# Bonus products from PSUM one step earlier, third convolution tile by full diagonals, and a reordered prologue in an RWKV-5 plus gated-convolution kernel

## The chip, the cores and the metric

The kernel runs on one core of a Trainium2 chip. The metric is device time in microseconds (us): the median over several executions. A profile of one execution gives its span, from the first to the last instruction, and the time of each instruction on the engines PE (TensorE, with PEld for its weight loads), DVE (VectorE), ACT (ScalarE), POOL (GpSimd) and SP (SyncE, which here only issues DMAs).

## What is computed

Two stages in fp32 at the edges: linear attention with a decaying state (B = 4 batches, H = 8 heads, S = 768 tokens, D = 48 per head), then a gated unit with a causal convolution over 5 tokens on the 384 concatenated channels.

```python
# attention, per token t
cur = einsum('bhd,bhe->bhde', u * k_t, v_t)          # the bonus
y_t = einsum('bhd,bhde->bhe', r_t, state + cur)
state = w * state + einsum('bhd,bhe->bhde', k_t, v_t)
# gated unit on x = y with heads concatenated: (4, 768, 384)
gate = sigmoid(sum_k conv_w[k] * shift(x, k))        # depthwise, causal, 5 taps
out = (gate * (x @ w_val)) @ w_out
```

## The kernel before

**Units.** Tokens are handled in chunks of 128, two chunks (256 tokens) to a unit, three units to a batch: 12 units. Decay within a chunk is folded into r and k: `dr` and `dk` hold powers of w, computed on ACT in the prologue as exp(scale x ln w). `scale_r` (L221) multiplies r by `dr`, one pair of heads of a whole batch at a time (POOL, in the prologue partly DVE); `scale_k` (L241) multiplies k of a unit by `dk` (POOL). PE transposes both: `transp_r` (L230) for one pair and one batch, `transp_k` (L256) for one unit, each into one of two PSUM buffers `tr_ps`, from which ACT (or DVE) copies to `rT` and `kT`.

**A step.** The order of all instructions is written out by hand in a loop of 13 steps (L511). Step i works on attention of unit i and on the gated unit of f = i - 1. Each engine executes its instructions in this order, one after the other. In step i:

- loads are issued on SP (k and v of unit i + 3; r of a later batch in steps 0, 2 and 5);
- `y_out(f)` (L364): the attention output of unit f on PE, transposed, from the state `z`, the masked scores `at` and the bonus term `dv`; ACT copies it to `xT`;
- `cast_v`, `scale_k` for unit i + 1 (ACT, POOL);
- `prod(i)` (L273): DVE multiplies `rT` by `kT`, both bf16 in SBUF, for the bonus of unit i;
- `attn(i, 0)` (L301): scores of the first chunk; `mask_at` (L318) on DVE; `bonus(i)` (L277): eight small matmuls that reduce the product, and a DVE copy to `s`; `bonus_v` (L293): POOL forms `dv` from v and `s`; `state` and `decay` (L327, L353): the new state on PE and its decay on DVE;
- `scale_r` of pairs of the next batch on POOL, by a small plan (L535): in most steps a pair is scaled one step before it is transposed, except in steps 1 and 2;
- `conv(f)` (L405), `value(f)` (L430) of the gated unit, with DVE's product `hT`;
- `attn(i, 1)`, its mask, state and decay;
- `transp_r` of one pair, `transp_k(i + 1)`, `project(f)` (L459) with ACT's copies `o_sb` and the output DMA, `transp_r` of a second pair.

**The gated unit.** The depthwise convolution is done on PE as matmuls with diagonal matrices. The 384 channels are three tiles of 128. Before, all diagonals are 64x64 (`cwdiag`), so four matmuls work at once on the quarters of the array: tiles 0 and 1 over 256 tokens, then tile 2 with its two chunks side by side (128 columns each). The two halves of a tile end up swapped by `qo = (q + i) % 2`, and the weights `wval` and `wout` are stored in a matching order: four column groups, tile 2 twice. Gate, value and `hT` are then two pieces of 384 columns. PSUM buffers for all of this come from a ring of three, `mm_ps`.

**The prologue.** It issues loads on SP (w, r of batch 0, k and v of the first units, the weights), small loads of w and u on POOL's queue, builds the identity and the mask on POOL, computes the decay factors on ACT, and lets PE multiply the identity 60 times (L492). Then it prepares unit 0: `scale_r`, `scale_k`, the transposes, `uw2` and `wcm` on DVE. The diagonals (`prep_conv`, L192) and the weights (`cast_weights`, L211) are prepared at the end of step 0.

Of the kernel before, what the change touches and what calls it, by code (L numbers as in the profile page):

```python
# [16 lines left out]
def kernel(  # L17
# [69 lines left out]
    nc.sync.dma_start(out=w_bc, in_=w.partition_broadcast(128))  # L87
    load_r(0)
    load_kv(0, "kv")
    load_kv(1, "k")  # L90

    nc.scalar.preload_act_table_set("natural_log_exp_and_others")
# [4 lines left out]
    for dst, src in ((wt, w), (ut, u)):  # L97
        for par in range(2):
            nc.gpsimd.dma_start(
                out=dst[64 * par : 64 * par + D, :],  # L100
                in_=src.rearrange("(p two) d -> two d p", two=2)[par],
            )

# [5 lines left out]
    ident = consts.tile([128, 128], BF16)  # L109
    make_identity(nc, ident)  # L110
# [18 lines left out]
    nc.scalar.activation(out=dk, in_=lnw_bc, func=AF.Exp, scale=sc_k)  # L129
    dr = consts.tile([128, H, J, D], F32)  # L130
    for j in range(J):
        nc.scalar.activation(
            out=dr[:, :, j, :], in_=lnw_bc, func=AF.Exp, scale=sc_r[:, j : j + 1]
        )
# [3 lines left out]
    nc.scalar.preload_act_table_set("sigmoid_and_others")  # L138
# [33 lines left out]

    wv_st = consts.tile([128, NT, DM], F32)
    wo_st = consts.tile([128, 4, DM], F32)
    cw5 = consts.tile([KW, DM], F32)

    def load_weights():
        nc.sync.dma_start(out=cw5, in_=moe_conv_w)
        nc.sync.dma_start(out=wv_st, in_=moe_w_val.rearrange("(t p) n -> p t n", p=128))
        wo = moe_w_out.rearrange("(t p) n -> p t n", p=128)  # L180
        nc.sync.dma_start(out=wo_st[:, 0::2, :], in_=wo[:, 0::2, :])
        nc.sync.dma_start(out=wo_st[64:128, 1::2, :], in_=wo[0:64, 1:3, :])
        nc.sync.dma_start(out=wo_st[0:64, 1::2, :], in_=wo[64:128, 1:3, :])

    wval = consts.tile([128, NT, 4, 128], BF16)
    wout = consts.tile([128, 4, DM], BF16)
    cw5b = consts.tile([KW, DM], BF16)
    cwT = consts.tile([128, NT, KW], F32)
    cwdiag = consts.tile([128, NT, KW, 64], BF16)
    eye = consts.tile([128, 64], BF16)  # L190

    def prep_conv():  # L192
# [10 lines left out]
        for T in range(NT):  # L203
            nc.vector.tensor_tensor(
                out=cwdiag[:, T],
# [3 lines left out]
            )  # L209

    def cast_weights():  # L211
        wv = wv_st.rearrange("p k (t x) -> p k t x", x=128)
        nc.gpsimd.tensor_copy(wval[:, :, 0::2, :], wv[:, :, 0::2, :])
        nc.gpsimd.tensor_copy(wval[:, :, 1::2, 64:128], wv[:, :, 1:3, 0:64])
        nc.gpsimd.tensor_copy(wval[:, :, 1::2, 0:64], wv[:, :, 1:3, 64:128])
        nc.scalar.copy(out=wout, in_=wo_st)
# [39 lines left out]
    def transp_k(n):  # L256
# [10 lines left out]
        )  # L267

# [4 lines left out]
    def prod(n):  # L273
        st["pr", n] = wk.tile([128, NP, W], BF16, name="pr")
        nc.vector.tensor_tensor(out=st["pr", n], in0=rTu(n), in1=st["kT", n], op=ALU.mult)  # L275
# [129 lines left out]
    def conv(n):  # L405
        b, cu = divmod(n, NU)
        xT, t0 = xT_t[b % 2], cu * W
        gate = ffn.tile([128, 2, W + C], BF16, name="gate")
        g_ps = [ps_mm.tile([128, W + C], F32, name="mm_ps") for i in range(2)]
        for T0 in (0, 2):  # L410
            for t in range(KW):
                for q in range(2):
                    for i in range(2):
                        T = 2 if T0 else i
                        c0, n0, o0 = (i * C, C, W) if T0 else (0, W, 0)
                        rows = slice(64 * q, 64 * q + 64)
                        qo = (q + i) % 2
                        nc.tensor.matmul(  # L418
                            out=g_ps[i][64 * qo : 64 * qo + 64, o0 : o0 + n0],
                            lhsT=cwdiag[rows, T, t, :],  # L420
                            rhs=xT[rows, T, t0 + c0 + t : t0 + c0 + t + n0],
                            start=(t == 0 and T0 == 0),
                            stop=(t == KW - 1),
# [164 lines left out]
```

## Time and profile before

| | |
|---|---|
| median of 13 runs (lowest to highest) | 119.01 us (118.57 to 120.05) |
| profiled execution: its time, its span | 118.78 us, 116.9 us |
| DVE product `pr` (L275), 12 times | 12.7 us, 0.68 to 2.24 each |
| DVE mask product (L320), 24 times | 29.2 us, 1.22 each |
| PE convolution (L418), 480 matmuls | 13.1 us busy |
| PE value (L437 and L446), 144 matmuls | 20.9 us busy |
| POOL `rs` (L223), 14 times | 20.5 us, 1.48 each |
| POOL waiting for `s_sb` from DVE | 35.7 us, 12 times |
| DMA, whole execution | 20.77 MB |

How to read it: a row of the timeline gives start, duration, engine, line and operation, then output and inputs with partitions x elements and type, then in brackets how long the engine had been idle and what ended that. Consecutive instructions of a kind are merged with their number. A wait row gives the total, the number and the longest. A stage row gives busy time and number of instructions per engine, the share of full clock that was granted to PE, the busy share of the DMA engines and their rate. The columns between the brackets and the shares stand in the order PE, PEld, DVE, ACT, POOL. Busy time of single PE instructions overlaps, since matmuls are pipelined; the start-to-start distance says what they cost.

Steps of the profiled execution begin (first matmul of `y_out`) at 22.73 (step 1), 34.98, 43.12, 50.30, 57.60, 65.35, 72.52, 79.82, 87.56, 94.80, 101.34 and 107.45 (step 12).

### The profile page before, as it was taken

The page shows a single profiled execution, that of the slowest core. Times are in us where ns is not written, and L with a number is a line of the kernel's source. Part 1 is how long each engine was busy: PE and PEld are TensorE (multiplying, and loading weights), DVE is VectorE, ACT ScalarE, POOL GpSimd, SP SyncE. Part 2 cuts the span into 40 slices and gives each one's busy share as a digit, 9 for nine tenths or more (in the row PEclk, how much of TensorE's full clock was granted, in tenths as well). Part 3 has the DMA queues.
Part 4 walks back from the last instruction along what each step waited for, and adds up shares of the span by engine and source line. Part 5 has one row for each costly group of instructions (what it writes and reads, how often), then busy time and mean ns, then how long its engine had stood idle before and what let it go on. Part 6 is the DMA issues. An engine that isn't in the chain of part 4 may idle for free.

```text
span 116.9 us, 5086 instructions
## 1 busy us (share of the span) xinstructions
PE 95.5 (82%) x2247; PEld 74.2 (63%) x2247; DVE 76.9 (66%) x122; ACT 69.1 (59%) x123; POOL 65.2 (56%) x62
## 2 busy tenths in 40 slices
PE   0397255867999698999979989998898999999860
PEld 0396233645778486768857776776776868776620
DVE  0508769898276717797797289977774778967030
ACT  4399250491259387393874964749669386644540
POOL 6948551962970990957939549299491825022000
PEclk9999965555599999999999999999999999999999
DMA  1899999899998999968869798993965003030303
GB/s 44 214 291 192 220 337 199 161 259 336 182 189 214 310 238 241 223 148 196 161 181 370 157 257 179 234 216 76 232 127 163 8 0 140 0 139 2 140 0 135
DMA packets 58719, 20.77 MB, mean 178 GB/s; under 512 B 50501, under 2 KB 58698, under 8 KB 58698
## 3 DMA queue, kind: packets, MB, share of 16 engines
q1 hardware_dynamic: 58570, 20.46, 72.2%
q8 instruction: 17, 0.28, 1.1%
q0 software_dynamic: 128, 0.00, 0.2%
q14 instruction: 4, 0.03, 0.1%
HBM read 15.74 MB, written 4.72 MB: 175 GB/s over the span
## 4 chain that ended last, share of the span: by engine, by line
PE 39%; SPq 15%; issue 12%; DVE 11%; ACT 9%; POOL 7%; DMA 3%; DVEq 0%; POOLq 0%; ACTq 0%
SPq L72 11%; PE mm_ps L418 8%; PE mm_ps L437 6%; DVE pr L275 6%; PE mm_ps L374 5%; PE mm_ps L466 5%; ACT kT L265 4%; POOL rs L223 3%; DMA k_st<-in_k_dram 3%; POOL ks L242 3%; DVE hT L454 3%; PE at_ps L308 3%; ACT o_sb L473 3%; PE mm_ps L282 3%; PE kv_ps L334 2%
## 5 line engine op out<-in xcount | busy, mean ns | idle before, releaser
L294 POOL TENSOR_TENSOR dv<-v_st,s_sb 128x768 bf16<-128x768 f32 x12 | 17.7, 1475 | 35.7 <-DVE s_sb L291 35.7
L320 DVE TENSOR_TENSOR at<-at_ps,mask 128x1024 bf16<-128x1024 f32 x24 | 29.2, 1218 | 3.0 <-PE at_ps L308 2.7
L454 DVE TENSOR_TENSOR hT<-mm_ps,gate 128x384 bf16<-128x384 f32 x24 | 13.4, 558 | 13.0 <-PE mm_ps L446 12.1
L223 POOL TENSOR_TENSOR rs<-r_st,dr 128x576 bf16<-128x576 f32 x14 | 20.5, 1480 | 2.1 <-ACT wct L136 2.1
L242 POOL TENSOR_TENSOR ks<-k_st,dk 128x768 bf16<-128x768 f32 x11 | 20.1, 1824 | 1.6 <-DMA k_st<-in_k_dram 1.6
L275 DVE TENSOR_TENSOR pr<-rT,kT 128x1024 bf16<-128x1024 bf16 x12 | 12.7, 1062 | 10.0 <-ACT rT L236 7.8
L427 ACT ACTIVATE gate<-mm_ps 128x384 bf16<-128x384 f32 x24 | 10.5, 488 | 13.0 <-PE mm_ps L418 13.0
L236 ACT COPY rT<-tr_ps 128x768 bf16<-128x768 bf16 x14 | 11.5, 818 | 10.1 <-PE tr_ps L235 10.1
L265 ACT COPY kT<-tr_ps 128x1024 bf16<-128x1024 bf16 x12 | 12.2, 1014 | 8.3 <-PE tr_ps L262 8.3
L466 PE MATMUL mm_ps<-wout,hT 128*128 128x384 bf16 x72 | 14.0, 327 | 0.5 <-DVE hT L454 0.3
L251 ACT CAST vb<-v_st 128x768 bf16<-128x768 f32 x12 | 10.4, 870 | 5.8 <-DMA v_st<-in_v_dram 5.8
L418 PE MATMUL mm_ps<-xT,cwdiag 64*64 64x256 bf16 (+1 forms) x480 | 13.1, 254 | 0.7 <-ACT xT L402 0.6
L418 PEld LDWEIGHTS <-cwdiag 64*64 64x64 bf16 x480 | 11.1, 111 | 2.9 <-issue 2.3
L473 ACT COPY o_sb<-mm_ps 128x384 f32<-128x384 f32 x24 | 10.7, 497 | 3.2 <-PE mm_ps L466 3.2
L437 PE MATMUL mm_ps<-xT,wval 128*128 128x256 bf16 x72 | 12.6, 285 | 0.0
L308 PE MATMUL at_ps<-rT,kT 48*128 48x128 bf16 x192 | 10.9, 232 | 1.0 <-DVE rT L236 0.6
L402 ACT CAST xT<-mm_ps 128x384 bf16<-128x384 f32 x24 | 11.3, 518 | 0.6 <-PE mm_ps L374 0.2
L359 DVE TENSOR_TENSOR z<-kv_ps,wcm 128x384 bf16<-128x384 f32 x20 | 10.9, 547 | 0.0
L235 PE MATMUL tr_ps<-ident,rs 128*128 128x128 bf16 x96 | 8.3, 225 | 2.4 <-POOL rs L223 1.7
L374 PE MATMUL mm_ps<-at,vb 128*32 128x128 bf16 x384 | 10.1, 227 | 0.0
L262 PE MATMUL tr_ps<-ident,ks 128*128 128x128 bf16 x96 | 7.8, 227 | 2.2 <-DVE ks L242 2.2
L493 PE MATMUL mm_ps<-ident 128*128 128x128 bf16 x60 | 5.4, 277 | 4.7 <-POOL ident masks.py:199 4.7
(67 smaller groups left out, 143.5 us busy)
## 6 DMA issues: line engine op xcount, KB each, us to landing
k_st<-in_k_dram SPq DMA_DIRECT2D x24, 192.0 KB, 5.1
v_st<-in_v_dram SPq DMA_DIRECT2D x24, 192.0 KB, 4.4
out_dram<-o_sb SPq DMA_DIRECT2D x11, 384.0 KB, 3.4
r_st<-in_r_dram SPq DMA_DIRECT2D x6, 576.0 KB, 4.9
r_st<-in_r_dram SPq DMA_DIRECT2D x4, 288.0 KB, 5.4
wv_st<-in_moe_w_val_dram SPq DMA_DIRECT2D x1, 576.0 KB, 4.2
wo_st<-in_moe_w_out_dram SPq DMA_DIRECT2D x1, 384.0 KB, 5.7
wo_st<-in_moe_w_out_dram SPq DMA_DIRECT2D x2, 192.0 KB, 5.7
```

The source lines that it names most:

```text
L223: eng.tensor_tensor(out=rs_t[p][:, :, :, 0:D].rearrange("p j a d -> p a j d"), in0=r_st[b][:, hs, :].rearrange("p a (j d) -> p a j d", d=D ...
L242: eng.tensor_tensor(out=ks_t[n % 3][:, :, :, :, 0:D].rearrange("p c n a d -> p c (n a) d"), in0=k_st[n], in1=dk[:, None, :, :].to_broadcas ...
L265: nc.scalar.copy(out=st["kT", n].rearrange("x n (c i) -> x c n i", c=U), in_=tr)
L275: nc.vector.tensor_tensor(out=st["pr", n], in0=rTu(n), in1=st["kT", n], op=ALU.mult)
L294: nc.gpsimd.tensor_tensor(out=dv_t[n % 2].rearrange("p c (h d) -> p (c h) d", d=D), in0=v_st[n].rearrange("p c h d -> p (c h) d"), in1=st[ ...
L308: nc.tensor.matmul(out=at_ps[:, par, p, :], lhsT=kT[rows, p, cs], rhs=rT[rows, p, cs], start=(p == 0), stop=(p == NP - 1), skip_group_chec ...
L320: nc.vector.tensor_tensor(out=st["at", n, cl].rearrange("p a n i -> p (a n) i"), in0=st["at_ps", n, cl].rearrange("p a n i -> p (a n) i"), ...
L374: nc.tensor.matmul(out=y_ps[32 * q : 32 * q + 32, T, :], lhsT=lt, rhs=rh, start=q not in first, stop=last, skip_group_check=True,)
L418: nc.tensor.matmul(out=g_ps[i][64 * qo : 64 * qo + 64, o0 : o0 + n0], lhsT=cwdiag[rows, T, t, :], rhs=xT[rows, T, t0 + c0 + t : t0 + c0 + ...
L437: nc.tensor.matmul(out=v_ps[:, 0:W], lhsT=wval[:, kt, i, :], rhs=xT[:, kt, t0 : t0 + W], start=(kt == 0), stop=(kt == NT - 1), skip_group_ ...
L454: nc.vector.tensor_tensor(out=hT[:, i], in0=v_ps, in1=st["gate", n][:, i], op=ALU.mult)
L466: nc.tensor.matmul(out=o_ps, lhsT=hT[:, i, c0 : c0 + C], rhs=wout[:, 2 + cl if j == 2 else i, :], start=(j == 0), stop=(j == 2),)
```

## The change

1. **Product.** `prod(i + 1)` is issued at the end of step i, and reads k from the PSUM buffer into which `transp_k` wrote it, not from ACT's copy `kT`. The copy stays, for `attn`.
2. **Gated unit.** Tiles 0 and 1 of the convolution stay as they were. Tile 2 is done with full 128x128 diagonals (`cwd2`) over the 256 columns: five matmuls. The pieces are tile 1 alone (256 columns) and tiles 0 and 2 together (512). `wval` and `wout` hold three groups, and 0.19 MB less of `w_out` is loaded. `prep_conv` is split: casting and transposing the taps, and the identity's halves, go to the start of unit 0's preparation; the diagonals (`prep_diag`) and `cast_weights` go into step 0, before its convolution slot.
3. **r preparation.** A table gives the pairs to be scaled and transposed per step. Batches 2 and 3 are prepared one step earlier than before, and r of batch 3 is loaded in step 4.
4. **Prologue.** The small loads of w and u go to ACT's queue; the identity is built first on POOL; `dr` is computed in two halves with `dk` between; all `scale_r` of batch 0 are on DVE; `uw2` and `wcm` go to POOL; the second table load of ACT comes later; the taps are loaded right after r; 110 idle matmuls in place of 60.

```diff
@@ prologue, after load_r(0)
+    nc.sync.dma_start(out=cw5, in_=moe_conv_w)
-            nc.gpsimd.dma_start(
+            nc.scalar.dma_start(
                 out=dst[64 * par : 64 * par + D, :],
...
-    nc.scalar.activation(out=dk, in_=lnw_bc, func=AF.Exp, scale=sc_k)
-    for j in range(J):
-        nc.scalar.activation(
-            out=dr[:, :, j, :], in_=lnw_bc, func=AF.Exp, scale=sc_r[:, j : j + 1]
-        )
+    for hh in range(2):
+        hs = slice(hh * NP, hh * NP + NP)
+        for j in range(J):
+            nc.scalar.activation(
+                out=dr[:, hs, j, :], in_=lnw_bc[:, hs], func=AF.Exp, scale=sc_r[:, j : j + 1]
+            )
+        if hh == 0:
+            nc.scalar.activation(out=dk, in_=lnw_bc, func=AF.Exp, scale=sc_k)
...
-    for _ in range(60):
-        nc.tensor.matmul(out=warm, lhsT=ident, rhs=ident, start=True, stop=True)
-    for p in range(NP):
-        scale_r(0, p, nc.gpsimd if p % 2 else nc.vector)
-    scale_k(0, nc.vector)
-    for p in range(2):
-        transp_r(0, p)
-    transp_k(0)
-    for p in range(2, NP):
-        transp_r(0, p, dve=True)
+    spin(110)
+    prep_conv()
+    scale_r(0, 0, nc.vector)
+    scale_r(0, 1, nc.vector)
+    transp_r(0, 0)
+    transp_r(0, 1)
+    scale_r(0, 2, nc.vector)
+    scale_k(0, nc.vector)
+    scale_r(0, 3, nc.vector)
+    transp_k(0)
+    transp_r(0, 2)
+    transp_r(0, 3, dve=True)
+    prod(0)
     cast_v(0)
@@ prep_diag (new)
+        for T in range(2):
+            nc.vector.tensor_tensor(
+                out=cwd[:, T],
+                in0=eye[:, None, :].to_broadcast([128, KW, 64]),
+                in1=cwT[:, T, :, None].to_broadcast([128, KW, 64]),
+                op=ALU.mult,
+            )
+        nc.vector.tensor_tensor(
+            out=cwd2,
+            in0=ident[:, None, :].to_broadcast([128, KW, 128]),
+            in1=cwT[:, 2, :, None].to_broadcast([128, KW, 128]),
+            op=ALU.mult,
+        )
@@ prod
-        nc.vector.tensor_tensor(out=st["pr", n], in0=rTu(n), in1=st["kT", n], op=ALU.mult)
+        nc.vector.tensor_tensor(
+            out=st["pr", n].rearrange("x n (c i) -> x c n i", c=U),
+            in0=st["tr", n],
+            in1=rTu(n).rearrange("x n (c i) -> x c n i", c=U),
+            op=ALU.mult,
+        )
@@ conv, second part
+        for t in range(KW):
+            nc.tensor.matmul(
+                out=g02[:, 1, :],
+                lhsT=cwd2[:, t, :],
+                rhs=xT[:, 2, t0 + t : t0 + t + W],
+                start=False,
+                stop=(t == KW - 1),
+                skip_group_check=True,
+            )
+        nc.scalar.activation(out=gate[:, 0, :], in_=g1, func=AF.Sigmoid)
+        nc.scalar.activation(out=gate[:, 1:3, :], in_=g02, func=AF.Sigmoid)
@@ value
+        for ts in (slice(0, 1), slice(1, 3)):
+            nt = ts.stop - ts.start
+            v_ps = ps_mm.tile([128, nt, W], F32, name="mm_ps")
+            for i in range(nt):
+                for kt in range(NT):
+                    nc.tensor.matmul(
+                        out=v_ps[:, i, :],
+                        lhsT=wval[:, kt, ts.start + i, :],
+                        rhs=xT[:, kt, t0 : t0 + W],
+                        start=(kt == 0),
+                        stop=(kt == NT - 1),
+                    )
@@ main loop
+    r_plan = {
+        1: (1, (0, 1), (0, 1)),
+        2: (1, (2, 3), (2, 3)),
+        3: (2, (0, 1), (0, 1)),
+        4: (2, (2, 3), (2, 3)),
+        5: (3, (0,), ()),
+        6: (3, (1, 2), (0, 1)),
+        7: (3, (3,), (2, 3)),
+    }
+    r_load = {0: 1, 2: 2, 4: 3}
...
         if ok(i):
-            prod(i)
             attn(i, 0)
...
+        if i == 0:
+            prep_diag()
+            cast_weights()
         if ok(f):
             conv(f)
...
-        if i == 0:
-            prep_conv()
-            cast_weights()
+        if ok(i + 1):
+            prod(i + 1)
```

## The prediction

> **What bounds the kernel now.** I read the page first, then busy time by stage, TensorE's waits, and the timeline around each wait.
>
> ```profile
> PE 95.5 (82%) x2247; PEld 74.2 (63%) x2247; DVE 76.9 (66%) x122; ACT 69.1 (59%) x123; POOL 65.2 (56%) x62
> ...
> PEclk9999965555599999999999999999999999999999
> ```
> ```profile
> 15.40:32.50 17.10, 12.51 (x200) 9.26 (x200) 13.18 (x25) 6.39 (x10) 10.06 (x9) 0.50 1.06 238
> 32.50:46.00 13.50, 11.90 (x324) 9.49 (x326) 7.77 (x12) 10.07 (x18) 7.84 (x6) 1.00 0.97 235
> 46.00:109.00 63.00, 60.13 (x1586) 46.36 (x1587) 47.86 (x68) 41.06 (x78) 36.68 (x24) 1.00 0.63 154
> ```
> (Columns: stretch, length, busy PE, weight loads, DVE, ACT, POOL, clock, DMA share, GB/s.) There are two regimes. From 46 to 109 us PE is busy 60.1 of 63.0 us at full clock: PE's own work is the bound, and only its remaining stalls can be won. Before 32.5 the granted clock is 0.5, DMA is full, and DVE (13.2 of 17.1) is busier than PE: the bound there is a serial chain.
>
> ```profile
> PE mm_ps L282 <- DVE pr L275: 5.9, 7, 1.9
> PE tr_ps L235 <- POOL rs L223: 1.7, 2, 1.0
> ```
> PE waits chiefly for the bonus product `pr`: 1.01 us (unit 0), 1.89 (unit 1), 0.50 (unit 3), and the other four together 2.5 (0.76 and 0.75 in units 5 and 8, the rest in 6 and 9). Two of them have this cause:
>
> ```profile
> 79.77 1.83 POOL L242 TENSOR_TENSOR ks<-k_st,dk 128x768 bf16<-128x768 f32 x1
> ```
> ```profile
> 79.92 2.23 DVE L275 TENSOR_TENSOR pr<-rT,kT 128x1024 bf16<-128x1024 bf16 x1 [0.62 <-ACT kT L265]
> 82.07 1.21 DVE L320 TENSOR_TENSOR at<-at_ps,mask 128x1024 bf16<-128x1024 f32 x1
> ```
> `pr` normally takes 0.69; here it ends at 82.15, 0.55 after POOL's `ks` ends at 81.60. It stood still until POOL was done. The mask product, which reads PSUM and one SBUF operand, took 1.21 to 1.23 us all 24 times, whatever POOL did.
>
> The start:
> ```profile
> 23.59 2.92 DVE L204 TENSOR_TENSOR cwdiag<-eye,cwT 128x320 bf16<-128x320 bf16 x3
> ...
> 26.43 0.68 DVE L275 TENSOR_TENSOR pr<-rT,kT 128x1024 bf16<-128x1024 bf16 x1
> ...
> 27.16 0.37 PE L282 MATMUL mm_ps<-uw,pr 128*128 128x2 bf16 x8 [1.89 <-DVE pr L275]
> ...
> 28.13 1.81 PE L418 MATMUL mm_ps<-xT,cwdiag 64*64 64x256 bf16 x40
> ```
> `prep_conv` occupies DVE from 22.17 to 26.51, in front of unit 1's product, and PE waits for it.
>
> **The change, part by part** (us, against the profiled execution: 118.78 with a span of 116.9. The median of the runs is 119.01, 0.23 above it).
>
> *Convolution and value, PE.* In the trace, groups of four 64x64 matmuls start 0.110 apart at 256 columns and 0.057 at 128; full-array matmuls of 256 columns start 0.109 apart; going from quarters to the full array costs 0.10 once. Before, unit 5: convolution 60.63 to 61.58 = 0.95; value to 62.82 = 1.24, in which the second half waits 0.145 for a PSUM buffer (its first start is 0.20 behind the last one, not 0.056). After: first two tiles 0.57, switch 0.10, five full diagonals 5 x 0.109 = 0.55, so 1.22; value nine x 0.109 = 0.98 plus the same 0.10 on leaving, 1.08. The buffer wait goes: the first gate (256 elements, about 0.38 from 0.49 for 384) now ends before the convolution's own last matmul. Sum 2.30 against 2.195: +0.10 a unit, eleven units: **+1.1**. PE is the bound, so all of it counts. DVE's `hT` pair costs 0.43 + 0.69 against 2 x 0.56, and ACT's gates 0.38 + 0.60 against 2 x 0.49: beside PE, nothing, except in the last unit, where the larger second piece comes later: **+0.15**.
>
> *The product from PSUM, one step earlier.* It no longer has two SBUF operands, so by the mask rows it should not stand behind POOL. In a step without r transposes the K transposes end near conv start + 3.6, ACT's kT copy (which the product's wait includes) near +4.8, and the next bonus matmuls come near +5.9; a product of 0.69 fits, behind `hT`, mask and decay. So the waits of units 5, 6, 8, 9 go: **-2.5**. Unit 3 keeps its 0.50: its product still needs the last rT copy, made by ACT at 43.81 to 44.66 after two o_sb copies. It is queued ahead of the next mask on DVE, so a late product delays mask, s, and POOL's dv.
>
> What does it take? No row of before has a bf16 product from PSUM. Nearest rows: 0.69 for the same elements and types from SBUF, 1.22 for 1,024 elements from PSUM in fp32. The Trainium skill disagrees with itself: "VectorE: DVE Perf Modes" (The perf-mode tier table) gives tensor_tensor with any PSUM operand one element a cycle, against two from SBUF. That speaks against this change. "PSUM — Partial Sum Buffer" (Specifications (TRN2)) says that tensor_tensor sends two at a time (0.52 ns an element) if 2-byte elements are adjacent in the output and in every tensor input, and asks nothing about where the inputs lie. All three operands here are bf16 with step 1, so I take 0.69. At 1.22 the extra 0.53 lies on the path at units 0, 1 and 3, and as about 0.2 each at units 10 and 11 (product ready at +6.0): 3 x 0.53 + 0.4 = +2.0. Below 0.69 there is nothing to gain: the copy of kT ends later than DVE is free.
>
> *r preparation one step earlier* (steps 3, 4, 6, 7 for 4, 5, 7, 8). The number of transposes is the same, but steps 3 and 4 now scale and transpose in one step, as steps 1 and 2 do already:
> ```profile
> 38.04 1.48 POOL L294 TENSOR_TENSOR dv<-v_st,s_sb 128x768 bf16<-128x768 f32 x1 [3.67 <-DVE s_sb L291]
> ...
> 39.48 2.76 POOL L223 TENSOR_TENSOR rs<-r_st,dr 128x576 bf16<-128x576 f32 x2
> ...
> 40.93 0.51 PE L235 MATMUL tr_ps<-ident,rs 128*128 128x128 bf16 x6 [1.00 <-POOL rs L223]
> ```
> The first rs ends 5.9 after the step began (34.98), since it stands behind dv, which waits for s. PE arrives at 5.2 in step 4, and in step 3 about 0.7 later because of unit 3's product: +0.7 and +0.45, **+1.15**. In steps 6 and 7 one rs is ready from the step before: nothing. r of batch 3 is loaded at step 4 for 5, when the DMA share is 0.6 to 0.9: nothing.
>
> *Prologue.* POOL no longer issues four DMAs (1.31 to 3.80) ahead of the identity, so the idle matmuls start near 1.45, not 4.69. Theirs is the first clock question:
> ```profile
> 8.00:8.50 0.50, 0.50 (x7) 0.50 (x6) 0.00 (x0) 0.00 (x0) 1.00 1.29 225
> ...
> 9.00:9.50 0.50, 0.50 (x13) 0.50 (x10) 0.00 (x0) 0.00 (x0) 1.00 1.09 179
> ```
> They run 0.107 apart until about 8.6, 3.9 us after the first, then 0.056, though the clock column says 1.00 throughout. The Trainium skill ("TensorE: Matmul & The Clock Gate", What's actually happening) has the clock come after a fully busy window of about 3.4 us that runs freely, so 3.4 to 6.8 us after the start; by the row alone, 3.9. By the row 110 of them end at 9.3; by the page between 9.2 and 10.8. I take the middle, 10.0 (before: 10.06). Behind them on PE are the cw5b transposes, behind those DVE's cwT and eye, and only then rs 0, rs 1, rs 2, ks 0: 10.0 + 0.25 + 0.65 + 3 x 0.7 + 0.9 = 13.9, against 13.86. The dr in halves (192 elements, about 0.36 each) would be ready near 7.6, but the queue hides it: nothing. DVE loses uw and wcm (17.34 to 18.00) to POOL, which is idle then: **-0.6** for the first product. The four small DMAs on ACT, at the 0.49 that SP's r issues take each, and the table load (1.28) end by 4.2, before w_bc lands (4.92): nothing. They share the completion slots with SP's, where each DMA waits for the eighth before it, so K of unit 0 starts some 1 us later, and 0.19 MB less of w_out (0.8 us at 235 GB/s) brings V of unit 1 back to its time (22.1).
>
> *Step 0.* The diagonals now stand before the second mask: 0.40 + 0.40 + 0.75, two SBUF operands, so the first waits for dv (20.02 to 21.50) and the others for a wval cast (about 0.35). 20.4 + 1.1 + 0.4 + 0.35 + 0.4 + 0.35 + 0.75 = 23.75, mask and decay 1.7, product 0.69: 26.1, less the 0.6 above, 25.5, against 27.11. The second half of y_out waits for that mask (about 24.3), and the convolution of unit 0 starts near 26.7, against 28.13. At half clock convolution and value cost 4.2 against 3.8, so 1.0 stays; without the 1.89 us hole PE may get its clock back up to 3 us earlier, which POOL's rs (behind r of batch 1, landing near 28) mostly takes back: 0.2. Together **-1.2**, between -0.3 (ACT's chain V cast, wout, kT late, or all locks lost) and -2.2.
>
> Sum: +1.1 + 0.15 - 2.5 + 1.15 - 1.2 = **-1.3**: 117.5 for the profiled execution, 117.7 for the median.
>
> **Rivals.** *One element a cycle from PSUM* (0.27): +2.0, so +0.7: 119.7, slower. Place: DVE's queue between decay and the next mask; it decides from about 1.05 us a product (1.3 / 3.6 exposed products above 0.69). For it: the tier table; against it: the PSUM page. *The idle matmuls hold DVE* (0.10): never sped up, they end at 1.45 + 110 x 0.107 = 13.2, all of rs and ks 3.2 later, 120.9. Against it: the speed-up 3.9 us in. *The start gives nothing* (0.18): diagonals and V as late as before, and POOL waits of 1.0 in both steps, as in step 2: -1.3 + 1.0 + 0.5 leaves 119.2, no change. It is also what follows if `pr` waits are replaced by waits on rs. My forecast: 0.45.
>
> **Numbers.** About 0.3% is what a measurement here can tell from no change. Faster, same, slower by case: forecast 0.42, 0.02, 0.01; tier table 0.05, 0.03, 0.19; no gain at the start 0.09, 0.07, 0.02; held DVE 0.02, 0.01, 0.07. Sums: 0.58, 0.13, 0.29. Range: from the large start gain (116.7) to the tier-table rival (119.7), each about 0.3 further, since the waits of steps 3 and 4 may be 1.0 each as in step 2, or may vanish where unit 3's product delays PE: 116.4 to 120.0.
>
> **What would show it.** `pr` rows of 0.69 (or 1.22), none near 2.2; PE's wait for `pr` only at units 0, 1 and 3; PE waiting for rs in steps 1 to 4; convolution plus value 2.30 at full clock; the convolution of unit 0 starting near 26.7; idle matmuls ending near 10. Wrong if these stand and the steps from 46 us on are still longer, or if ks of unit 0 comes after 14.5.

## The result, and the profile after

The changed kernel takes 117.82 us (median of 11 runs, 116.67 to 118.24) against 119.11 for the kernel before in the same comparison: a ratio of 0.988 (95% interval 0.985 to 0.991), 1.2% faster. The forecast was 117.7. The profiled execution took 118.15, with a span of 116.2. Ratios here leave disturbed runs out and medians do not, so the two can differ a little.

To see where the time went I cut both spans at the first `y_out` matmul of step 3 ("the third step" from here on). From there on PE has its full clock, and a step lasts the same within 0.03 us in every kernel that has the same code for it, apart from rare standstills of PE (see the end); I call this the steady part. What lies ahead of it I call the start. It varies between executions: step 2 begins at 34.13 here, but at 33.60 and 33.65 in two kernels below that have the same code up to there, and the 11 runs of the changed kernel spread over 1.6 us.

| us | before | after | difference |
|---|---|---|---|
| start: the third step begins at | 43.12 | 42.27 | -0.85 |
| steady part | 73.75 | 73.89 | +0.14 |
| span | 116.87 | 116.16 | -0.71 |

So by the profile the steady part gained nothing, and all of the gain is in the start. By the medians the start gained 1.29 + 0.14 = 1.4.

The page of the changed kernel; DVE is less busy (chiefly since it no longer stands still in a product), PE more:

```profile
PE 100.0 (86%) x2081; PEld 77.0 (66%) x2081; DVE 70.5 (61%) x119; ACT 72.1 (62%) x130; POOL 60.9 (52%) x60
...
PEclk9999855587699999999999999999999999999999
```

The same three stretches as before the change, then two half microseconds of the idle matmuls:

```profile
15.40:32.50 17.10, 12.99 (x201) 9.47 (x199) 11.58 (x17) 9.21 (x13) 12.05 (x10) 0.64 1.03 239
32.50:46.00 13.50, 12.02 (x312) 9.27 (x309) 8.11 (x13) 10.45 (x19) 7.57 (x6) 1.00 0.96 237
46.00:109.00 63.00, 60.75 (x1424) 45.88 (x1421) 42.84 (x66) 42.03 (x77) 36.42 (x24) 1.00 0.63 155
6.50:7.00 0.50, 0.50 (x8) 0.50 (x6) 0.00 (x0) 0.50 (x2) 0.00 (x0) 1.00 1.08 316
7.50:8.00 0.50, 0.50 (x13) 0.50 (x11) 0.00 (x0) 0.50 (x2) 0.16 (x1) 1.00 0.92 253
```

In the start DVE is 1.6 us less busy and POOL 2.0 busier; afterwards PE is as full as it was. The idle matmuls begin at 1.35, speed up at 7.08 and end at 10.4 (forecast 10.0).

PE's waits for `rs` and for the product, in the changed kernel:

```profile
PE tr_ps L246 <- POOL rs L234: 1.8, 3, 0.9
...
PE mm_ps L299 <- DVE pr L287: 1.2, 3, 0.5
```

The wait for the product went from 5.9 us in seven places to 1.2 in three; the one for `rs` is 1.8 in three places (0.89 in step 2, 0.50 and 0.40 in steps 3 and 4).

The product of unit 5, which took 2.24 us before:

```profile
58.05 1.02 ACT L276 COPY kT<-tr_ps 128x1024 bf16<-128x1024 bf16 x1
58.07 1.82 POOL L253 TENSOR_TENSOR ks<-k_st,dk 128x768 bf16<-128x768 f32 x1
...
59.10 0.69 DVE L287 TENSOR_TENSOR pr<-tr_ps,rT 128x1024 bf16<-128x1024 bf16 x1 [1.06 <-ACT kT L276]
```

It starts in the middle of POOL's `ks` and still takes 0.69. It also starts no earlier than before: it waits for ACT's `kT` copy out of the same PSUM buffer, and step 5 begins at 59.00. The product precedes that step in the order of the program, not in time.

The start:

```profile
21.50 2.07 DVE L208 TENSOR_TENSOR cwd<-eye,cwT 128x320 bf16<-128x320 bf16 x2
23.50 0.96 DVE L214 TENSOR_TENSOR cwd<-ident,cwT 128x640 bf16<-128x640 bf16 x1
...
24.38 1.21 DVE L337 TENSOR_TENSOR at<-at_ps,mask 128x1024 bf16<-128x1024 f32 x1
...
25.64 0.41 PE L391 MATMUL mm_ps<-at,vb 128*32 128x128 bf16 x16 [1.25 <-DVE at L337]
...
25.98 0.68 DVE L287 TENSOR_TENSOR pr<-tr_ps,rT 128x1024 bf16<-128x1024 bf16 x1
...
26.71 0.35 PE L299 MATMUL mm_ps<-uw,pr 128*128 128x2 bf16 x8 [0.16 <-DVE pr L287]
...
27.35 1.12 PE L434 MATMUL mm_ps<-xT,cwd 64*64 64x256 bf16 x20
```

The hole of 1.89 us in front of unit 1's bonus matmuls is 0.16. In its place PE waits 1.25 a little earlier, in `y_out`, for the mask that now stands behind the diagonals (the forecast had PE there at 24.3; it is 25.64). That is the forecast's mechanism, but its first part failed: unit 0's product starts at 19.22, 1.2 later than before, in place of 0.6 earlier.

### The profile page after: what moved, and what is told of

The parts are those of the page before. It is cut to its first block, busy times and chain, and to the rows that moved or that the text cites. A ratio compares the mean times of both kernels' runs of the same rounds, so it can differ in the third digit from the quotient of the medians.

```text
span 116.2 us, 4768 instructions
## 1 busy us (share of the span) xinstructions
PE 100.0 (86%) x2081; PEld 77.0 (66%) x2081; DVE 70.5 (61%) x119; ACT 72.1 (62%) x130; POOL 60.9 (52%) x60
## 4 chain that ended last, share of the span: by engine, by line
PE 44%; POOL 20%; issue 14%; ACT 12%; DVE 6%; POOLq 0%; ACTq 0%; DVEq 0%
POOL rs L234 8%; PE mm_ps L508 8%; PE mm_ps L464 7%; POOL ks L253 6%; PE mm_ps L391 5%; PE mm_ps L434 5%; PE mm_ps L483 5%; PE mm_ps L443 5%; ACT rT L247 3%; ACT o_sb L490 3%; ACT kT L276 3%; POOL dv L311 3%; PE at_ps L325 3%; PE tr_ps L273 3%; ACT xT L419 2%
## 5 line engine op out<-in xcount | busy, mean ns | idle before, releaser
L471 DVE TENSOR_TENSOR hT<-mm_ps,gate 128x256 bf16<-128x256 f32 (+1 forms) x24 | 13.4, 558 | 15.3 <-PE mm_ps L464 15.3
L247 ACT COPY rT<-tr_ps 128x768 bf16<-128x768 bf16 x15 | 12.3, 817 | 13.6 <-PE tr_ps L246 13.6
L234 POOL TENSOR_TENSOR rs<-r_st,dr 128x576 bf16<-128x576 f32 x12 | 16.6, 1402 | 0.0
L464 PE MATMUL mm_ps<-xT,wval 128*128 128x256 bf16 x108 | 14.5, 281 | 0.0
L287 DVE TENSOR_TENSOR pr<-tr_ps,rT 128x1024 bf16<-128x1024 bf16 x12 | 8.3, 691 | 7.0 <-ACT kT L276 3.7
L464 PEld LDWEIGHTS <-wval 128*128 128x128 bf16 x108 | 10.9, 101 | 1.8
L262 ACT CAST vb<-v_st 128x768 bf16<-128x768 f32 x12 | 10.4, 870 | 1.8 <-DMA v_st<-in_v_dram 1.8
L246 PEld LDWEIGHTS <-rs 128*128 128x128 bf16 x96 | 6.8, 104 | 7.0 <-POOL rs L234 2.5
L434 PE MATMUL mm_ps<-xT,cwd 64*64 64x256 bf16 x240 | 9.3, 281 | 1.1 <-ACT xT L419 0.6
L508 PE MATMUL mm_ps<-ident 128*128 128x128 bf16 x110 | 9.0, 265 | 1.4 <-POOL ident masks.py:199 1.4
L508 PEld LDWEIGHTS <-ident 128*128 128x128 bf16 x110 | 8.9, 124 | 1.4 <-POOL ident masks.py:199 1.4
```

What stands on the lines that cost most here:

```text
L234: eng.tensor_tensor(out=rs_t[p][:, :, :, 0:D].rearrange("p j a d -> p a j d"), in0=r_st[b][:, hs, :].rearrange("p a (j d) -> p a j d", d=D ...
L246: nc.tensor.transpose(tr[:, j, :], rs_t[p][:, j].rearrange("p a x -> p (a x)"), ident)
L247: (nc.vector.tensor_copy if dve else nc.scalar.copy)(out=st["rT", b][:, p, :].rearrange("x (p j) -> x p j", j=J), in_=tr.rearrange("x j p ...
L434: nc.tensor.matmul(out=g[64 * qo : 64 * qo + 64], lhsT=cwd[rows, T, t, :], rhs=xT[rows, T, t0 + t : t0 + t + W], start=(t == 0), stop=(t = ...
L464: nc.tensor.matmul(out=v_ps[:, i, :], lhsT=wval[:, kt, ts.start + i, :], rhs=xT[:, kt, t0 : t0 + W], start=(kt == 0), stop=(kt == NT - 1),)
L508: nc.tensor.matmul(out=t_, lhsT=ident, rhs=ident, start=True, stop=True)
```

## The experiments

Each is the changed kernel with one edit, unless it says otherwise. "Steady" and "third step" are from its profiled execution, the ratio is that to the kernel before. A long edit is shown in part; `...` marks what is left out. Three questions: what did PSUM do for the product, what did each edit cost or bring in the steady part, and what sets the start.

### The product

**SBUF again, same place.**

```diff
-            in0=st["tr", n],
+            in0=st["kT", n].rearrange("x n (c i) -> x c n i", c=U),
```

> The changed kernel (median 117.82 us, 0.988 of the kernel before), with the product moved to the end of the preceding step as there, but reading k from SBUF (kT) as before. Theory A, that the two SBUF operands are what made the product stand behind POOL: in the steps where POOL still scales r at the end of the step (1 to 4, 6 and 7) several pr rows take 1.5 to 2.5 us in place of 0.69, PE's wait for pr grows from 1.2 us to 3 to 5, and the time is 118.8 to 120.3 (0.998 to 1.010 of before). Theory B, that taking the product one step earlier is what removed the waits and PSUM adds nothing: pr rows stay at 0.69, the time is within 0.3 us of 117.8. A third outcome is a gain: K's PSUM transpose buffer is released by the kT copy instead of by the product, so the fourth r transpose of the start comes 1.2 us sooner; if that is larger than the locks, 117.0.

118.64 us, 0.998 (0.993 to 1.002): the change's gain is gone. Steady 74.37, 0.48 more than in the changed kernel. Products of units 1, 4, 5, 6 and 7 take 1.57, 1.34, 1.34, 1.53 and 2.09. The one of unit 7 shows it; then comes PE's wait there:

```profile
71.30 1.82 POOL L253 TENSOR_TENSOR ks<-k_st,dk 128x768 bf16<-128x768 f32 x1
...
71.58 2.09 DVE L287 TENSOR_TENSOR pr<-kT,rT 128x1024 bf16<-128x1024 bf16 x1 [0.49 <-ACT kT L276]
...
73.72 0.35 PE L299 MATMUL mm_ps<-uw,pr 128*128 128x2 bf16 x8 [0.68 <-DVE pr L287]
```

Theory A holds: it is the operand in SBUF that makes the product stand behind POOL. Less of it lies on the path than forecast (PE's wait for products is 2.7, not 3 to 5), since most of these products had slack. The steady part accounts for 0.48 of the 0.8 us by which the median is longer. In the start PE waits 1.05 for unit 1's product, in place of 0.16, but this profiled execution was the fastest of its 12 (117.56), so its third step, at 40.83, says little. The third outcome (an earlier start, since K's PSUM buffer is released sooner) is not in the median. In the trace unit 0's product starts at 17.09 in place of 19.22, but 1.15 of these 2.1 us are there already at the first `rs` (10.02 in place of 11.17), since the idle matmuls sped up sooner; about 1.0 is left for the buffer.

**The kernel before, product alone from PSUM** (issued at the end of the preceding step; r plan, convolution and start as before).

```diff
-        nc.vector.tensor_tensor(out=st["pr", n], in0=rTu(n), in1=st["kT", n], op=ALU.mult)
+        nc.vector.tensor_tensor(
+            out=st["pr", n].rearrange("x n (c i) -> x c n i", c=U),
+            in0=st["tr", n],
+            in1=rTu(n).rearrange("x n (c i) -> x c n i", c=U),
+            op=ALU.mult,
+        )
...
-            prod(i)
...
             cast_weights()
+        if ok(i + 1):
+            prod(i + 1)
```

> The kernel before with one edit: the product reads k from the PSUM transposes and is issued at the end of the preceding step. Its steady part (from the first y_out matmul of the third step to the end of the span, all at full clock) is 73.8 us in the kernel before and 73.9 in the changed one. The prediction's term of -2.5 for units 5, 6, 8, 9 gives a steady part of 71.3 and a time of 116.5 (0.979 of before). Rival: only units 5 and 8 (0.76 and 0.75) stood behind POOL; units 6 and 9 waited 0.5 for the copy of their last r transposes, as unit 3 does, which this edit leaves: -1.5, a steady part of 72.3 and 117.5 (0.987).

118.13 us, 0.994 (0.990 to 0.998). All products take 0.69. Steps 5 and 8, whose products stood behind POOL, last 7.07 each in place of 7.75 and 7.74; step 9, which holds the wait of unit 9, lasts 7.17 as before, and step 6 longer:

```profile
66.48 0.69 DVE L276 TENSOR_TENSOR pr<-tr_ps,rT 128x1024 bf16<-128x1024 bf16 x1 [2.23 <-ACT rT L236]
...
67.13 0.34 PE L380 MATMUL mm_ps<-ident,dv 128*32 128x128 bf16 x10 [1.04 <-issue]
```

Unit 6's product waits for the copy of its last `rT`, which reading k from PSUM doesn't touch. The rival holds: the product is worth 0.68 + 0.67 = 1.35, not 2.5. (PE also stood still for 1.04 us with its inputs ready, see the end, which lengthened this step by 0.51; without that the steady part is 73.07 - 0.51 = 72.56, so 1.19 less than before: the other steps together lost 0.16.)

### The steady part

**The r plan and r loads of before.**

```diff
-        3: (2, (0, 1), (0, 1)),
-        4: (2, (2, 3), (2, 3)),
-        5: (3, (0,), ()),
-        6: (3, (1, 2), (0, 1)),
-        7: (3, (3,), (2, 3)),
+        3: (2, (0,), ()),
+        4: (2, (1, 2), (0, 1)),
+        5: (2, (3,), (2, 3)),
+        6: (3, (0,), ()),
+        7: (3, (1, 2), (0, 1)),
+        8: (3, (3,), (2, 3)),
     }
-    r_load = {0: 1, 2: 2, 4: 3}
+    r_load = {0: 1, 2: 2, 5: 3}
```

> The changed kernel with the r preparation and r loads of before (batches 2 and 3 scaled and transposed over three steps, 4, 5 and 7, 8). The prediction's term: PE's waits for rs in steps 3 and 4 (0.50 and 0.40 us in this kernel's trace) go and no pr wait comes in their place, because the product no longer stands behind POOL: 0.9 us less, 116.9 (0.981 of before). Rival: the waits for pr at units 6 and 9 come back, since their r is transposed at the end of steps 5 and 8, right before the product: 0.5 each, so 117.6 to 118.0 (0.987 to 0.990).

117.28 us, 0.985 (0.979 to 0.991), which overlaps the changed kernel. The steady part settles it: 73.82 against 73.89. PE's waits from 29 us on:

```profile
PE mm_ps L299 <- DVE pr L287: 1.5, 3, 0.5
PE tr_ps L246 <- POOL rs L234: 0.9, 1, 0.9
```

0.9 of `rs` waits is gone and 1.0 of product waits (units 6 and 9, behind unit 3) is back. The new plan trades the one for the other.

**Quarters in the gated unit again** (`conv`, `value`, `project`, `wval`, `wout` and the weight loads of before, that part of the change read backwards).

```diff
-    cwd = consts.tile([128, 2, KW, 64], BF16)
-    cwd2 = consts.tile([128, KW, 128], BF16)
+    cwdiag = consts.tile([128, NT, KW, 64], BF16)
...
-    wval = consts.tile([128, NT, NT, 128], BF16)
-    wout = consts.tile([128, NT, DM], BF16)
+    wval = consts.tile([128, NT, 4, 128], BF16)
+    wout = consts.tile([128, 4, DM], BF16)
```

> The changed kernel with the gated unit of before: third convolution tile and its values in 64x64 quarters, four weight groups (and the weight loads that go with it). The prediction's term (+0.10 a unit over eleven units, +0.15 in the last): 1.25 us less than the changed kernel, so 116.6 us, 0.978 of before; convolution plus value 2.20 us at full clock in place of 2.30. Rival 1, PE waits elsewhere take it back (rs, hT or xT come no sooner because PE arrives sooner): 117.2 to 117.8 (0.984 to 0.988). Rival 2, the new form also costs something that the two intervals do not show (steps 10 and 11 last 0.15 and 0.3 longer than before, more than 0.10): 115.8 to 116.2 (0.972 to 0.976).

117.61 us, 0.981 (0.974 to 0.988). Steady 72.92, so 0.97 less; steps 2 to 6 gain nothing (in 2 to 4 PE waits longer for `rs`, 2.1 in place of 1.8), steps 7 to 10 gain 0.10 to 0.13 each, step 11 0.24, the tail 0.3. With the r plan of before, where such waits are absent, the same edit is worth 73.82 - 72.56 = 1.26. But the median moved by only 0.2 (0.8 by the ratios), so by the medians the start got longer. V of unit 1 is cast as soon as it has landed, at 23.59 in place of 21.05:

```profile
23.59 0.83 ACT L254 CAST vb<-v_st 128x768 bf16<-128x768 f32 x1 [5.64 <-DMA v_st<-in_v_dram]
```

The 0.19 MB more of the four-group weights lie ahead of it. In all five traces with these loads ahead of it, the kernel before included, the cast starts at 22.1 to 23.6; in the seven with three groups whose ACT waits for this V it starts at 20.6 to 21.8, and at 20.36 in the last run below, which loads the extra pieces behind V.

**POOL's `rs` ahead of `dv`, from step 2 on.**

```diff
             bonus(i)
+            if i > 1:
+                for p in sp:
+                    scale_r(rb, p, nc.gpsimd)
             bonus_v(i)
...
-        for p in sp:
-            scale_r(rb, p, nc.gpsimd)
+        if i == 1:
+            for p in sp:
+                scale_r(rb, p, nc.gpsimd)
```

> The changed kernel with POOL's rs of steps 2 to 7 issued before dv in place of behind it. Theory, the first rs is late only because it stands behind dv, which waits for s: the waits for rs of steps 2, 3 and 4 (0.89, 0.50, 0.40) go and no pr wait comes back: 1.8 us less, 116.0 (0.974 of before), steady part 73.0. Rival: dv, now 2.9 us later, holds the next y_out or makes the next ks late, so the waits turn into waits for dv or ks: 117.3 to 118.2 (0.985 to 0.993).

115.32 us, 0.964 (0.957 to 0.971). Steps 2, 3 and 4 last 7.18, 7.96 and 7.51 in place of 8.14, 8.64 and 8.09, and PE waits for `rs` nowhere:

```profile
42.52 2.77 POOL L234 TENSOR_TENSOR rs<-r_st,dr 128x576 bf16<-128x576 f32 x2 [2.58 <-DMA r_st<-in_r_dram]
45.25 1.47 POOL L311 TENSOR_TENSOR dv<-v_st,s_sb 128x768 bf16<-128x768 f32 x1
46.60 0.50 PE L246 MATMUL tr_ps<-ident,rs 128*128 128x128 bf16 x6
```

In the changed kernel POOL had been idle for 2.67 in front of `dv`, waiting for `s`; now it does both `rs` first, as soon as r has landed. The theory holds: the three steps are 2.2 shorter. Step 5 is 0.69 longer, 0.47 of it a standstill of PE with its inputs ready (see the end), so the steady part is 73.45 and the span 1.9 shorter. (The profiled execution, 116.29, was the slowest of six.)

### The start

**The start alone** (quarters, r plan and weights as before, product from SBUF at the start of its own step; only the prologue and the place of the diagonals are those of the change).

```diff
         if ok(i):
+            if i > 0:
+                prod(i)
             attn(i, 0)
...
-        if ok(i + 1):
-            prod(i + 1)
```

> The changed kernel's start (idle matmuls, DMA order, prologue, diagonals ahead of the second mask) with everything else as before: quarters in the gated unit and its four-group weights, r plan of before, product from SBUF at the start of its own step (unit 0's at the end of the start). If the start and the steady part add up as the prediction summed them, the steady part is 73.8 as before and all of the change's gain is here: the third step begins 0.85 sooner, at 42.3, and the time is 118.0 (0.992). Rival: the start's gain needs the product from PSUM, since unit 1's product would stand behind POOL otherwise (1.57 in place of 0.68 in the SBUF-product run): third step at 43.1 or later, 118.8 to 119.3 (0.998 to 1.002).

118.18 us, 0.995 (0.990 to 1.000). Third step at 43.13, steady 73.56. Unit 1's product takes 2.02 behind POOL's `ks` and PE waits 1.4 for it. The rival holds in the trace; in the runs some 0.6 of the gain is left. So moving the diagonals is not enough. Two things of the changed start are missing here, the product that POOL doesn't hold and the smaller weights (V of unit 1 is cast at 22.78), and this run doesn't tell them apart. Median less steady part, a rough measure of the start, is 45.4 before, 43.9 in the changed kernel, 44.3 with the SBUF product alone, 44.7 with the four-group weights alone and 44.6 with both. That points to the weights more than to the product, but the differences are hardly clear of the noise, so it is not shown.

**60 idle matmuls in place of 110.**

```diff
-    spin(110)
+    spin(60)
```

> The changed kernel with 60 idle matmuls in place of 110. In the changed kernel they end at 10.4 us, and DVE's first rs stands behind cwT, which PE makes only after them. Theory A, the queue behind the idle matmuls sets the start: they end near 7.8, cw lands at 8.8, the first rs starts near 9.6 in place of 11.2, ks of unit 0 ends near 12.9 in place of 14.4, and up to 1.5 us is gained, of which V of unit 1, the clock and POOL's r take back some: 116.5 to 117.3 (0.978 to 0.985). Theory B, the clock is what the idle matmuls buy: without the last 2.6 us of them the granted clock falls to half earlier than 13.9 us, transposes of the start run at half, and what is gained on DVE is lost on PE: 117.6 to 118.4 (0.987 to 0.994).

116.29 us, 0.976 (0.971 to 0.981): by the medians the changed kernel lost about 1.5 us to its own idle matmuls. They end at 6.2, `cw` lands at 8.8, and the first `rs` starts at 9.90 in place of 11.17. In the changed kernel, then here:

```profile
11.17 2.38 DVE L234 TENSOR_TENSOR rs<-r_st,dr 128x576 bf16<-128x576 f32 x3
```
```profile
8.76 0.35 DVE L195 CAST cw5b<-cw 5x384 bf16<-5x384 f32 x1 [5.28 <-DMA cw<-in_moe_conv_w_dram]
9.43 0.17 DVE L201 CAST cwT<-mm_ps 128x15 f32<-128x15 bf16 x1 [0.32 <-PE mm_ps L198]
...
9.90 2.24 DVE L234 TENSOR_TENSOR rs<-r_st,dr 128x576 bf16<-128x576 f32 x3
```

Theory A, but the queue behind them explains the 1.5 only in part. How long it is held depends on when the idle matmuls speed up. In the changed kernel's trace that came latest of all; in five other traces with 110 of them and the same order the first `rs` starts at 10.02 to 10.45, so 0.12 to 0.55 after 9.90. Where the rest of the 1.5 comes from is open.

**Start order**: `rs` and `ks` ahead of the convolution's preparation, r transposes ahead of K's.

```diff
-    prep_conv()
     scale_r(0, 0, nc.vector)
     scale_r(0, 1, nc.vector)
     transp_r(0, 0)
     transp_r(0, 1)
     scale_r(0, 2, nc.vector)
-    scale_k(0, nc.vector)
     scale_r(0, 3, nc.vector)
-    transp_k(0)
+    scale_k(0, nc.vector)
     transp_r(0, 2)
     transp_r(0, 3, dve=True)
+    transp_k(0)
+    prep_conv()
     prod(0)
```

> The changed kernel with another order in the start: all four rs and ks of unit 0 ahead of the convolution's preparation on DVE (cw5b, cwT, eye), r transposes ahead of the K transposes on PE; idle matmuls stay at 110. Theory, two things that the prediction missed or priced at zero cost the start: DVE's rs stand behind cwT, which stands behind the idle matmuls, and the fourth r transposes wait 1.16 us for an r copy because K's PSUM buffer is held until the product reads it. Then the first rs starts near 8.5 in place of 11.2, the first product near 16.5 in place of 19.2, and the third step begins 1.5 to 2.5 sooner: 115.3 to 116.3 (0.968 to 0.977). Rival: V of unit 0, K of unit 1 and the weights land when they land, and what is gained at the first product is lost before the third step: less than 0.5 gained, 117.3 to 117.8 (0.985 to 0.989).

117.00 us, 0.986 (0.981 to 0.992). The first product starts at 15.04, 4.2 sooner, and the third step at 41.62, 0.65 sooner. The median lies between the two forecasts; most of the 4.2 is lost again, as the rival has it. ACT shows where it went:

```profile
21.67 0.83 ACT L262 CAST vb<-v_st 128x768 bf16<-128x768 f32 x1 [4.79 <-DMA v_st<-in_v_dram]
...
23.46 1.00 ACT L276 COPY kT<-tr_ps 128x1024 bf16<-128x1024 bf16 x1
...
24.52 0.61 PE L325 MATMUL at_ps<-rT,kT 48*128 48x128 bf16 x8 [1.92 <-ACT kT L276]
```

ACT stands 4.79 at V of unit 1, while the `kT` copy that PE needs is queued behind it, its transposes long done.

**The start-order kernel with one idle matmul.**

```diff
-    spin(110)
+    spin(1)
```

> The start-order kernel (median 117.0 us, third step at 41.6 in its trace) with one idle matmul in place of 110. DVE no longer stands behind them there, so this shows what the idle matmuls buy by themselves. Theory A, they buy the clock: without them PE runs at half speed from its first transposes on, and no full-clock window comes before about 30 us; first product about 0.7 later, third step about 1 us later, 117.8 to 118.5 (0.989 to 0.995 of before). Theory B, the start is set by data landing, DVE and ACT, and PE's speed is covered: within 0.4 of 117.0 (0.979 to 0.986). A gain is possible if early PE work of a half-clock stretch counts against later windows: 116.3.

116.79 us, 0.983 (0.979 to 0.988), against 117.00 with 110. PE runs at half speed from its first transposes (K's start 0.107 apart, as the idle matmuls did before they sped up) until 28.73, and it costs nothing: theory B. The third step begins at 40.12, even sooner than with 110. What sets this start instead is, by the waits in the trace, data landing, DVE and ACT.

**The start-order kernel with ACT's casts late** (V of unit 1 and the output weights, moved to step 1 behind the `xT` copies).

```diff
+            if i == 1:
+                cast_v(1)
+                nc.scalar.copy(out=wout, in_=wo_st)
+            if i > 0:
+                cast_v(i + 1)
-            cast_v(i + 1)
...
-        nc.scalar.copy(out=wout, in_=wo_st)
```

> The start-order kernel with V of unit 1 and the output weights cast on ACT in step 1, behind the xT copies of unit 0, in place of ahead of unit 1's kT copy. In the start-order trace ACT stood 4.79 us at V of unit 1, which landed at 21.7, and kT of unit 1 (transposes done at 19.1) was copied at 23.5; PE waited 1.92 for it. Theory, ACT's order is what ate the 4.2 us that the first product had gained: kT of unit 1 near 20.2, product near 22.5, convolution of unit 0 near 23.5 in place of 26.2; r of batch 1 (landing near 28.9) takes part of it back, so the third step begins 1 to 1.5 sooner, near 40.4: 115.7 (0.971). Rival, r of batch 1 takes all of it back: 116.8 to 117.2 (0.980 to 0.984), with PE's wait for rs in step 1 of 2 us or more.

117.67 us, 0.985 (0.979 to 0.992), against 117.00 and 0.986 with the start order alone: no gain. Unit 1's product starts at 21.81 and the convolution of unit 0 at 24.45, 1.8 sooner than with the start order alone, and the third step still begins at 41.63. Neither theory: PE doesn't wait for `rs` in step 1, but ACT stands again, 2.52 at V of unit 2, with unit 0's gates behind it (PE waits 0.86 for them), and PE was at half speed until 31.70.

### Together

**Quarters, `rs` ahead of `dv` and the start order**, and three more edits in the start: casts late, diagonals behind unit 1's product, r of batch 1 loaded ahead of V of unit 2. The 110 idle matmuls stay, though 60 had gained.

```diff
-        if i == 0:
-            load_kv(2, "v")
         if i in r_load:
             load_r(r_load[i])
+        if i == 0:
+            load_kv(2, "v")
...
+        if i == 0:
+            prep_diag()
```

> All edits that gained, in one kernel: the changed kernel with quarters in the gated unit, rs ahead of dv on POOL, start order and late ACT casts, the diagonals behind unit 1's product in step 0, and r of batch 1 loaded ahead of V of unit 2. If they add up (118.0 less 1.0 for the quarters, 1.8 to 2.5 for rs, 0.8 for the start order, 1.2 for ACT): 112.3 to 113.5 (0.943 to 0.953). Rival, the start is held by r of batch 1 or V of unit 1 whatever the order, and the quarters' gain goes into waits elsewhere: 114 to 115 (0.957 to 0.966).

118.70 us, 0.990 (0.986 to 0.995): worse than both forecasts, and the trace points to one edit, the new order of the two loads.

```profile
31.31 0.83 ACT L253 CAST vb<-v_st 128x768 bf16<-128x768 f32 x1 [5.98 <-DMA v_st<-in_v_dram]
32.05 0.86 ACT L435 ACTIVATE gate<-mm_ps 128x384 bf16<-128x384 f32 x2
```

V of unit 2 lands behind r of batch 1, ACT stands 5.98 at its cast, and PE waits 5.7 for the gates. The steady part is 72.27 all the same, with 1.5 us in which PE stood still with its inputs ready.

**Three edits**: 60 idle matmuls, `rs` ahead of `dv`, quarters with the two extra weight pieces loaded and cast late.

```diff
     load_kv(2, "k")
+    load_weights2()
-    spin(110)
+    spin(60)
...
             transp_k(i + 1)
+        if i == 0:
+            nc.scalar.copy(out=wout[:, 1::2, :], in_=wo_st[:, 1::2, :])
```

> The changed kernel with three edits that each gained by its trace: 60 idle matmuls (116.3 us alone), rs ahead of dv on POOL (115.3 alone), and quarters in the gated unit, whose two extra pieces of the output weights (0.19 MB) are loaded behind V of unit 1 and K of unit 2 and cast behind unit 1's kT, so that they don't push V of unit 1 back as they did in the quarters run (cast at 23.6 in place of 21.1). If they add up: 1.5 for the idle matmuls, 2.5 for rs, 1.0 for the quarters, so 112.8 (0.947), with a steady part of 72.3 and the third step near 39.8. Rival, the quarters' gain is absorbed in waits and V of unit 2, 0.8 us later now, takes back the start: 114.0 to 114.8 (0.957 to 0.964).

115.11 us (113.42 to 115.57), 0.972 (0.966 to 0.977). The profiled execution took 113.42, the fastest of six, and is near what was expected: third step at 39.92, steady 71.73. The median isn't, and can't be told from `rs` ahead of `dv` alone (115.32). Both beat the kernel before and the changed one.

## Why the prediction was right, point by point

The time and the sign were right, and so was the split: -0.1 forecast for the steady part and -1.2 for the start, +0.14 and -0.85 in the profile (-1.4 by the medians). Of the steps behind it some were wrong, and cancelled. In the steady part the runs give the three terms one by one: product -1.19 (forecast -2.5), gated unit +1.26 (+1.25), r plan +0.07 (+1.15), in sum the +0.14. The errors of the first and the last term are largely one mistake: 1.0 us of waits was booked for the product that the r plan removes. That the rest cancelled too, and that the start came out near -1.2 by another way, is luck.

- **Product at 0.69 from PSUM**: right, 0.68 to 0.69 twelve times. Of the two rules of the Trainium skill that the prediction weighed, the one in "VectorE: DVE Perf Modes" (The perf-mode tier table), by which the forecast had it at 1.22, doesn't hold for this instruction; the one in "PSUM — Partial Sum Buffer" (Specifications (TRN2)) does.
- **It no longer stands behind POOL**: right, shown by the SBUF run (up to 2.09).
- **"The waits of units 5, 6, 8, 9 go: -2.5"**: they went, for two reasons that the prediction took for one. Units 5 and 8 are worth 1.35 and are the product's (0.16 of it is lost in other steps). The 0.5 each of units 6 and 9 is the late copy of the last `rT`, as in unit 3, and is the r plan's: it moves the r transposes of batches 2 and 3 into steps that aren't followed at once by the batch that needs them.
- **r plan +1.15**: the two waits were 0.50 and 0.40, so 0.9 (step 4 forecast at 0.7, since PE arrived later there). With the 1.0 that it takes away, its net is +0.07.
- **Convolution and value +1.1 + 0.15**: right, step by step. In steps 3 to 11 the convolution takes 1.23 and the value 1.08 (forecast 1.22 and 1.08) against 0.95 and 1.24 before. The sum is 1.26 where nothing absorbs it, of which 0.26 is in step 11, where PE waits 0.26 for the larger `hT` piece, as was forecast for the last unit alone. In the changed kernel 0.3 of it is covered by the `rs` waits, so 0.97. What the prediction priced at next to nothing is its other side: 0.19 MB less of weights, which brings V of unit 1 to ACT sooner.
- **First product 0.6 earlier**: wrong, 1.2 later. `ks` of unit 0 ended at 14.42, not 13.9, chiefly since the idle matmuls ended at 10.4 and not at 10.0 (the 9.3 that the prediction works out from the row of before should have been 9.5), and the step missed a wait. With two PSUM buffers and K's held until the product has read it, the fourth r transposes must wait until ACT has emptied the other one:

```profile
17.32 0.80 PE L246 MATMUL tr_ps<-ident,rs 128*128 128x128 bf16 x6 [1.16 <-ACT rT L247]
```

- **Unit 1's product ready at 25.5, convolution of unit 0 at 26.7**: 26.66 and 27.35, against 27.11 and 28.13 before. Mechanism right, size half or less. K of unit 0 was issued later, as forecast (6.24 in place of 3.19, once r had landed at 6.22), but landed no later (10.67 against 10.90), and V of unit 1 landed sooner (cast at 21.05 against 22.10). PE waited for `rs` in steps 2 to 4 as forecast, but not in step 1.
- **Rivals**: one element a cycle is excluded by the rows. "The idle matmuls hold DVE" was given for the case that they never speed up; they did, and held DVE all the same, for 1.3 us in this trace (first `rs` at 11.17 against 9.90): so both it and my sum were true in part. "The start gives nothing" is what the new start nearly gives with the product from SBUF and the larger weights.

## What to carry to other kernels

Before a wait is credited to an edit, find for each instance what ended it: two of these four waits for the same product had another cause, which a second edit removed. An operation in the order of a queue is not placed in time by it: what the queue's head waits for (V's landing in front of `kT`, `s` in front of `rs`, idle matmuls in front of `cwT`) sets everything behind, and putting work that is ready ahead of work that waits was worth more here (2.5 us by the medians, 1.9 by the spans) than anything in the change. And an edit that gains engine time in a stretch bound by data landing moves the hole rather than closing it; look for the next wait before counting the gain.

## What was not expected of the hardware

- **The clock changes on a grid of its own.** In every trace PE's granted clock changes at times a multiple of 3.413 us apart, with a different offset in each. The idle matmuls sped up 2.8 us after their start in one trace and 5.7 in another; the final return to full clock lay between 28.1 and 32.7 and the third step between 39.9 and 43.4 (leaving out the kernel with the new order of loads). That is a free-running window, as the Trainium skill has it ("TensorE: Matmul & The Clock Gate", What's actually happening). The prediction took from that page that a whole window must be busy first, so at least 3.4 us; in five of the 13 traces with idle matmuls the clock came after 2.8 to 3.1. The window is the likely reason (argued, not shown) why the start varies by a microsecond, so that starts of single profiles can't be compared to better than that. The clock column reads 1.00 ahead of the first change even where matmuls run at half speed.
- **PE can run out of instructions.** In five traces PE stands still with its inputs ready: 1.04 us in the run of the product alone, 0.47 in that of `rs` ahead of `dv`, 0.58 and 0.96 in that with the new order of loads, 0.31 in the last run, and once in that with one idle matmul, where step 5 is 0.46 longer. The changed kernel has none. The second of these, and the queue of PE's instructions on the page of the same run:

```profile
61.72 0.34 PE L325 MATMUL at_ps<-rT,kT 48*128 48x128 bf16 x5 [0.47 <-issue]
```
```profile
q8 instruction: 16, 0.26, 1.0%
```

Its 16 packets of 16 KB for some 4,170 instructions of PE and PEld are one for every 256 or so. Counted from the start of the trace, the six standstills come after 1,217, 1,729, 1,985 (three times) and 2,241 instructions, which all differ by multiples of 256, and each ends 1.25 to 1.59 us after a packet has landed. If a packet is taken for each such block of 256, PE never begins a block sooner than 1.24 us after its packet in any of the 218 blocks of all traces. So PE was waiting for its next instructions. The six packets had started late: 1.8 to 4.1 us after PE began the block before, against 0.9 in the median. Why they did is open, as is the spread of some 2 us among the runs of the two fastest kernels.
